# Turning attention scores onto their keys' partitions with a VectorE block transpose instead of TensorE transposes, with whole-chunk K buffers

## The chip, the cores and the metric

The kernel runs on one core of a Trainium2 chip. The metric is the time of one launch on the device, in microseconds (us). A core has five engines, which run side by side: TensorE (PE; its weight loads are listed apart as PEld), VectorE (DVE), ScalarE (ACT), GpSimd (POOL) and SyncE (SP, which here only issues DMA transfers). Sixteen DMA engines move data from memory (HBM) into SBUF. Matmul results land in PSUM.

## The reference, cut to what matters

One token is decoded: layer norm, attention over a cache of 65,536 keys with 32 query heads on 4 key/value heads, output projection, then layer norm and a gated feed-forward block.

```python
# x: 1x1x1024; k_cache, v_cache: 1x4x65536x128, bf16
q = x_normed @ wq                                    # 32 heads of 128
scores = einsum("bhqd,bhkd->bhqk", q, k) * 128**-0.5
p = softmax(scores)
o = einsum("bhqk,bhkd->bhqd", p, v)                  # then @ wo, + x
h2 = h + (gelu(hn @ w_gate) * (hn @ w_up)) @ w_down
```

K and V are 67 MB each, the weights about 39 MB. All of it must be read once: 173 MB.

## The kernel before: the parts that matter

All large loads share one pool of `NBUF = 5` buffers of 4 MB each. A load is issued when the buffer it reuses has been read for the last time.

```python
CW = 16384; NBUF = 5
chpool = ctx.enter_context(tc.tile_pool(name="chpool", bufs=NBUF))
def load(src, name):
    t = chpool.tile([P, CW], BF16, name=name, tag="ch")
    ...
    nc.sync.dma_start(out=tv, in_=src)
```

A K buffer is worked in four chunks of 32 keys per partition. Each chunk is transposed on TensorE (two neighbouring bf16 values of a key travel as one fp32 element), four blocks at a time into a PSUM bank, and copied out ("evicted") by ScalarE or VectorE. Then the query is multiplied with it. After two chunks the scores lie along the columns of a PSUM bank and have to be turned, so that each partition holds the scores of its own keys:

```python
for c in range(NBK):                                   # NBK = NB2 = 4
    kt_ps = ps_kt.tile([P, NB2, P], F32, ...)          # 3 PSUM banks
    for b in range(NB2):
        m0 = b * 8 + c * 2 + hf
        nc.tensor.transpose(out=kt_ps[:, b, :], in_=k32s[m0 // 16][:, m0 % 16, :], identity=ident_f[:])
    kt_sb = ktpool.tile([P, NB2, P], F32, ...)         # 6 buffers
    # evict kt_ps -> kt_sb on ACT or DVE
...
for par in range(2):
    for c in range(NBK):                               # column group c reads tile c
        nc.tensor.matmul(qk_ps[32*c:32*c+32, :], lhsT=qsel[:, g, par, hf, :], rhs=mv[:, :, :, par], ...)
...                                                    # after the second chunk of a pair:
nc.scalar.copy(out=qk_sb[:], in_=qk_ps[:])
for b in range(NB2):
    nc.tensor.transpose(out=sct_ps[:, b, :], in_=qk_sb[:, b*P:(b+1)*P], identity=ident_f[:])
nc.vector.tensor_copy(out=sl.rearrange("p h (m t) -> p m t h", t=2), in_=src_v)
nc.vector.tensor_reduce(out=st["mx"][:, :, pi], in_=sl, axis=AX.X, op=ALU.max)
```

When a head's K is done, the maximum is spread over the partitions and 16 exponentials on ScalarE make the probabilities. The V chunks of a head are interleaved with the K chunks of the next head.

## Time and profile before

| | before |
|---|---|
| time, median of the first 3 runs | 412.56 us (412.27 to 413.38) |
| span of the profiled run | 410.4 us |
| DMA bytes, mean rate | 173.43 MB, 423 GB/s |
| busy: PE, PEld, DVE, ACT | 296.6, 194.9, 168.2, 168.0 us |
| K load, issue to landing (median) | 27.3 us |

No engine's busy share says what bounds this kernel. The first thing to read is a table by stretch. The lines below, from the table of windows of the kernel before, give for each stretch (us from the start) its length, then the busy time of PE, PEld, DVE, ACT and POOL with instruction counts, then the granted TensorE clock (1.00 is full speed), the mean busy share of the 16 DMA engines, and what they moved in GB/s.

```profile
10.00:400.00 390.00, 290.19 (x2576) 189.71 (x2580) 165.87 (x283) 168.04 (x281) 3.57 (x7) 0.88 1.00 431
330.00:400.00 70.00, 38.63 (x353) 21.25 (x349) 7.11 (x29) 1.39 (x3) 2.17 (x4) 0.66 0.99 428
```

The DMA engines are busy throughout at 431 GB/s, and at nearly the same rate (428) from 330 to 400 us, where the other engines do little. So the rate does not come from what the engines do. (Single 10 us windows read up to 465 GB/s, with a DMA share of up to 1.08, so only long stretches are compared here.)

Whether the queue ever runs empty is the next question. These are the DMA issues of the page (size of one, median us from issue to landing).

```profile
k_sb<-in_A_k_cache_dram SPq DMA_DIRECT2D x16, 4096.0 KB, 27.3
v_sb<-in_A_v_cache_dram SPq DMA_DIRECT2D x16, 4096.0 KB, 21.7
```

A 4 MB load takes 4.19 MB / 431 GB/s = 9.7 us of the stream but 22 to 27 us from issue to landing, so it usually stands behind one or two others. How close it comes to running empty is read from the issues in order of time. This is the SP queue's timeline in head 0 (start, duration, transfer):

```profile
45.50 0.33 SPq L94 DMA_DIRECT2D v_sb<-in_A_v_cache_dram  x1
59.18 0.33 SPq L94 DMA_DIRECT2D k_sb<-in_A_k_cache_dram  x1
73.72 0.33 SPq L94 DMA_DIRECT2D v_sb<-in_A_v_cache_dram  x1
88.28 0.33 SPq L94 DMA_DIRECT2D k_sb<-in_A_k_cache_dram  x1
105.21 0.33 SPq L94 DMA_DIRECT2D v_sb<-in_A_v_cache_dram  x1
```

The stream needs a new load every 9.7 us. In head 0, where only K is worked, buffers come free every 13.7 to 14.6 us, and the fifth comes 17 us after the fourth: it waits for the first V matmuls, which wait for head 0's exponentials. The prefetched loads are the reserve that pays for this. I counted landings at 9.9 us per load from the start. By that count the load issued at 105.21 came about 6 us before the stream would have run dry.

Finally, the costliest groups (line, engine, operation, output<-inputs, shapes, count | busy us, mean ns | idle time before them and who ended it). Here and below, lines L223 to L321 are those of the kernel before.

```profile
L223 PE MATMUL kt_ps<-ident_f,k_sb 128*128 128x128 f32 x1024 | 148.2, 288 | 17.3 <-DVE kt_sb L230 12.9 <-DMA k_sb<-in_A_k_cache_dram 4.1 <-ACT kt_sb L228 0.2
...
L230 DVE COPY kt_sb<-kt_ps 128x1024 bf16<-128x1024 bf16 x140 | 94.7, 687 | 76.1 <-PE qk_ps L248 42.5 <-PE kt_ps L223 30.7
L248 PE MATMUL qk_ps<-kt_sb,qsel 128*32 128x512 bf16 x512 | 65.0, 395 | 7.7 <-DVE kt_sb L230 7.7
L259 DVE COPY sc_sb<-sct_ps 128x512 f32<-128x512 f32 x32 | 34.1, 1066 | 46.0 <-PE sct_ps L256 43.7 <-ACT kt_sb L228 2.3
...
L286 ACT ACTIVATE pT<-sc_sb,nbias 128x256 bf16<-128x256 f32 x64 | 31.5, 493 | 20.5 <-DVE nbias L278 20.5
L260 DVE TENSOR_REDUCE mx<-sc_sb 128x8 f32<-128x512 f32 x32 | 22.0, 687 | 1.0
L256 PE MATMUL sct_ps<-ident_f,qk_sb 128*128 128x128 f32 x128 | 19.9, 278 | 8.6 <-ACT qk_sb L253 8.6
L253 ACT COPY qk_sb<-qk_ps 128x512 f32<-128x512 f32 x32 | 18.8, 589 | 24.9 <-PE qk_ps L248 16.5 <-PE o_ps L319 8.3
```

L253, L256 and L259 are the three steps that turn the scores. L230 shows evictions that wait 42.5 us for QK matmuls: with six small buffers, the third and fourth eviction of a chunk need a buffer that the previous chunk's QK still reads.

The chain of waits (the work that ended last, followed back), by engine:

```profile
PE 52%; DMA 24%; DVE 14%; ACT 7%; issue 2%; SPq 0%; DVEq 0%; ACTq 0%
```

### The profile page before, as it was taken

The page shows a single profiled execution, that of the slowest core. Times are in us where ns is not written, and L with a number is a line of the kernel's source. Part 1 is how long each engine was busy: PE and PEld are TensorE (multiplying, and loading weights), DVE is VectorE, ACT ScalarE, POOL GpSimd, SP SyncE. Part 2 cuts the span into 40 slices and gives each one's busy share as a digit, 9 for nine tenths or more (in the row PEclk, how much of TensorE's full clock was granted, in tenths as well). Part 3 has the DMA queues.
Part 4 walks back from the last instruction along what each step waited for, and adds up shares of the span by engine and source line. Part 5 has one row for each costly group of instructions (what it writes and reads, how often), then busy time and mean ns, then how long its engine had stood idle before and what let it go on. Part 6 is the DMA issues. An engine that isn't in the chain of part 4 may idle for free.

```text
span 410.4 us, 6350 instructions
## 1 busy us (share of the span) xinstructions
PE 296.6 (72%) x2704; PEld 194.9 (47%) x2704; DVE 168.2 (41%) x296; ACT 168.0 (41%) x281; POOL 5.1 (1%) x16
## 2 busy tenths in 40 slices
PE   0438989889688987496988929888987466366366
PEld 0216656655366654464566617455654223163134
DVE  0213565557256545255556535456545101021011
ACT  0013766653855654733655634455744700000000
POOL 1100000000000000000000000000000001000000
PEclk9986999999999999599999966999999585668565
DMA  8999999999999999999999999999999999999994
GB/s 358 409 460 407 460 408 457 407 456 412 439 428 423 444 423 442 422 442 410 449 420 444 417 447 420 428 440 414 454 410 453 415 449 418 434 433 436 424 420 172
DMA packets 6684, 173.43 MB, mean 423 GB/s; under 512 B 896, under 2 KB 896, under 8 KB 1152
## 3 DMA queue, kind: packets, MB, share of 16 engines
q1 hardware_dynamic: 6496, 173.02, 98.1%
q8 instruction: 21, 0.34, 0.3%
q14 instruction: 7, 0.06, 0.0%
q10 hardware_dynamic: 160, 0.00, 0.0%
HBM read 173.02 MB, written 0.00 MB: 422 GB/s over the span
## 4 chain that ended last, share of the span: by engine, by line
PE 52%; DMA 24%; DVE 14%; ACT 7%; issue 2%; SPq 0%; DVEq 0%; ACTq 0%
PE kt_ps L223 27%; PE qk_ps L248 11%; DMA wd_sb<-in_B_w_down_dram 9%; DMA k_sb<-in_A_k_cache_dram 7%; DMA wo_sb<-in_A_wo_dram 7%; DVE sc_sb L259 6%; PE acc_ps L303 5%; ACT pT L286 5%; PE sct_ps L256 4%; DVE mx L260 4%; DVE kt_sb L230 3%; ACT qk_sb L253 2%; PE at_ps L361 1%; PE o_ps L319 1%; PE d_ps L361 1%
## 5 line engine op out<-in xcount | busy, mean ns | idle before, releaser
L223 PE MATMUL kt_ps<-ident_f,k_sb 128*128 128x128 f32 x1024 | 148.2, 288 | 17.3 <-DVE kt_sb L230 12.9
L228 ACT COPY kt_sb<-kt_ps 128x1024 bf16<-128x1024 bf16 x116 | 116.4, 1013 | 91.7 <-PE kt_ps L223 63.1
L223 PEld LDWEIGHTS kt_ps<-ident_f,k_sb 128*128 128x128 f32 x1024 | 117.6, 147 | 55.5 <-issue 21.3
L230 DVE COPY kt_sb<-kt_ps 128x1024 bf16<-128x1024 bf16 x140 | 94.7, 687 | 76.1 <-PE qk_ps L248 42.5
L248 PE MATMUL qk_ps<-kt_sb,qsel 128*32 128x512 bf16 x512 | 65.0, 395 | 7.7 <-DVE kt_sb L230 7.7
L259 DVE COPY sc_sb<-sct_ps 128x512 f32<-128x512 f32 x32 | 34.1, 1066 | 46.0 <-PE sct_ps L256 43.7
L286 ACT ACTIVATE pT<-sc_sb,nbias 128x256 bf16<-128x256 f32 x64 | 31.5, 493 | 20.5 <-DVE nbias L278 20.5
L303 PE MATMUL acc_ps<-v_sb,pT 128*32 128x512 bf16 x512 | 33.8, 408 | 3.8 <-DMA v_sb<-in_A_v_cache_dram 3.8
L253 ACT COPY qk_sb<-qk_ps 128x512 f32<-128x512 f32 x32 | 18.8, 589 | 24.9 <-PE qk_ps L248 16.5
L248 PEld LDWEIGHTS <-qsel 128*32 128x32 bf16 x512 | 15.1, 94 | 26.2 <-issue 23.9
L256 PE MATMUL sct_ps<-ident_f,qk_sb 128*128 128x128 f32 x128 | 19.9, 278 | 8.6 <-ACT qk_sb L253 8.6
L303 PEld LDWEIGHTS <-pT 128*32 128x32 bf16 x512 | 14.7, 102 | 18.7 <-issue 7.2
L260 DVE TENSOR_REDUCE mx<-sc_sb 128x8 f32<-128x512 f32 x32 | 22.0, 687 | 1.0
L256 PEld LDWEIGHTS sct_ps<-ident_f,qk_sb 128*128 128x128 f32 x128 | 14.3, 141 | 13.6 <-ACT qk_sb L253 13.6
L172 ACT COPY wg_ev<-wg_ps 96x512 f32<-96x512 f32 x1 | 0.6, 582 | 45.9 <-PE wg_ps L165 45.9
L312 PE MATMUL l_ps<-lpart,ones_f 128*128 128x8 f32 x16 | 3.7, 306 | 15.7 <-ACT pT L286 15.6
L165 PE MATMUL wu_ps<-wu_sb,hnz 128*32 128x512 bf16 x56 | 7.1, 620 | 9.7 <-DMA wu_sb<-in_B_w_up_dram 9.7
L165 PEld LDWEIGHTS <-hnz 128*32 128x32 bf16 x112 | 4.8, 123 | 17.8 <-issue 15.6
L361 PE MATMUL at_ps<-wo_sb,o2z 128*32 128x512 bf16 x64 | 6.6, 590 | 8.6 <-DMA wo_sb<-in_A_wo_dram 8.6
L286 ACT ACTIVATION_READ_ACCUMULATOR pT<-sc_sb,nbias 128x1 f32 x64 | 11.9, 187 | 0.0
L172 ACT ACT_TABLE_LOAD x1 | 1.3, 1283 | 25.0 <-DVE q_ev L170 25.0
L312 PEld LDWEIGHTS l_ps<-lpart,ones_f 128*128 128x128 f32 x16 | 3.0, 234 | 17.8 <-ACT pT L286 17.4
(125 smaller groups left out, 97.7 us busy)
## 6 DMA issues: line engine op xcount, KB each, us to landing
k_sb<-in_A_k_cache_dram SPq DMA_DIRECT2D x16, 4096.0 KB, 27.3
v_sb<-in_A_v_cache_dram SPq DMA_DIRECT2D x16, 4096.0 KB, 21.7
wq_sb<-in_A_wq_dram SPq DMA_DIRECT2D x2, 4096.0 KB, 16.7
wo_sb<-in_A_wo_dram SPq DMA_DIRECT2D x2, 4096.0 KB, 29.7
wg_sb<-in_B_w_gate_dram SPq DMA_DIRECT2D x2, 3584.0 KB, 33.1
wu_sb<-in_B_w_up_dram SPq DMA_DIRECT2D x2, 3584.0 KB, 40.6
wd_sb<-in_B_w_down_dram SPq DMA_DIRECT2D x1, 3584.0 KB
wd_sb<-in_B_w_down_dram SPq DMA_DIRECT2D x1, 1792.0 KB, 29.6
```

Source lines behind the costliest of these rows:

```text
L165: nc.tensor.matmul(banks[s // 4][32 * g:32 * g + 32, :], lhsT=stat, rhs=mov(s), start=first, stop=last, tile_position=(0, 32 * g))
L223: nc.tensor.transpose(out=kt_ps[:, b, :], in_=k32s[m0 // 16][:, m0 % 16, :], identity=ident_f[:])
L228: nc.scalar.copy(out=dst_bf, in_=src_bf)
L230: nc.vector.tensor_copy(out=dst_bf, in_=src_bf)
L248: nc.tensor.matmul(qk_ps[32 * c:32 * c + 32, :], lhsT=qsel[:, g, par, hf, :], rhs=mv[:, :, :, par], start=(hf == 0 and par == 0), stop=(hf ...
L253: nc.scalar.copy(out=qk_sb[:], in_=qk_ps[:])
L256: nc.tensor.transpose(out=sct_ps[:, b, :], in_=qk_sb[:, b * P:(b + 1) * P], identity=ident_f[:])
L259: nc.vector.tensor_copy(out=sl.rearrange("p h (m t) -> p m t h", t=2), in_=src_v)
L260: nc.vector.tensor_reduce(out=st["mx"][:, :, pi], in_=sl, axis=AX.X, op=ALU.max)
L286: nc.scalar.activation(out=pT[:, :, r, :], in_=sc_sb[:, r, hf * HG * TG:(hf + 1) * HG * TG].rearrange("p (a t) -> p a t", t=TG), func=ACT. ...
L303: nc.tensor.matmul(acc[32 * c:32 * c + rep * TG, :], lhsT=pTs[a // HG][:, a % HG, :, :].rearrange("p r t -> p (r t)"), rhs=v_sb[:, i * TG: ...
L361: nc.tensor.matmul(bank[32 * g:32 * g + 32, :], lhsT=stat, rhs=w2[:, s * 512:(s + 1) * 512], start=first, stop=last, tile_position=(0, 32 ...
```

## The change

The intent is to turn the scores with one VectorE 32x32 block transpose straight from PSUM. For that, column group c of the QK matmuls takes the keys of partitions 32c to 32c+31 of the whole chunk, so that the block transpose puts each score on its own partition. This drops a ScalarE copy, four TensorE transposes and the strided VectorE copy per pair of chunks, and frees a PSUM bank, which goes to the K transposes. Each chunk now has one large buffer, two in rotation. The scores lie key by key with the 8 heads side by side, so the maximum and the exponentials read at a step of 32 bytes. To make room in SBUF a small selector (`osel`) shares memory with the query tile and is built after attention.

```diff
-    ktpool = actx.enter_context(tc.tile_pool(name="ktpool", bufs=6))
+    ktpool = actx.enter_context(tc.tile_pool(name="ktpool", bufs=2))
-    ps_kt = actx.enter_context(tc.tile_pool(name="ps_kt", bufs=3, space=PSUM))
+    ps_kt = actx.enter_context(tc.tile_pool(name="ps_kt", bufs=4, space=PSUM))
-    ps_sct = actx.enter_context(tc.tile_pool(name="ps_sct", bufs=1, space=PSUM))
...                                        (osel moved; o_sb to another pool)
+        kt = ktpool.tile([P, NBK * NB2, P], F32, name="kt_sb", tag="kt")
-                m0 = b * 8 + c * 2 + hf
+                m0 = (c * NB2 + b) * 2 + hf
...
-            st["sc_sb"] = scpool.tile([P, rep, NT], F32, name="sc_sb", tag="sc")
+            st["sc_sb"] = scpool.tile([P, NT, rep], F32, name="sc_sb", tag="sc")
...
-                nc.tensor.matmul(qk_ps[32 * c:32 * c + 32, :], lhsT=qsel[:, g, par, hf, :], rhs=mv[:, :, :, par],
+                nc.tensor.matmul(qk_ps[32 * c:32 * c + 32, :], lhsT=qsel[:, g, par, hf, :],
+                                 rhs=mv[:, :, 32 * c:32 * c + 32, par],
...
-        nc.scalar.copy(out=qk_sb[:], in_=qk_ps[:])
-        for b in range(NB2):
-            nc.tensor.transpose(out=sct_ps[:, b, :], in_=qk_sb[:, b * P:(b + 1) * P], identity=ident_f[:])
-        nc.vector.tensor_copy(out=sl.rearrange("p h (m t) -> p m t h", t=2), in_=src_v)
-        nc.vector.tensor_reduce(out=st["mx"][:, :, pi], in_=sl, axis=AX.X, op=ALU.max)
+        sl = sc_sb[:, 2 * pi * CH:(2 * pi + 2) * CH, :]
+        nc.vector.transpose(out=sl.rearrange("p n h -> p (n h)"), in_=qk_ps[:])
+        nc.vector.tensor_reduce(out=st["mx"][:, :, pi], in_=sl.rearrange("p n h -> p h n"), axis=AX.X, op=ALU.max)
...
-                                     in_=sc_sb[:, r, hf * HG * TG:(hf + 1) * HG * TG].rearrange("p (a t) -> p a t", t=TG),
+                                     in_=sc_sb[:, hf * HG * TG:(hf + 1) * HG * TG, r].rearrange("p (a t) -> p a t", t=TG),
```

More of the change, by code (lines that the diff above doesn't have):

```diff
@@ L57 @@
     W2 = 2 * rep
-    assert NT % (DCH * CH) == 0 and CH % TG == 0 and CH == 32 and W2 == 16 and DCH % 2 == 0
+    assert NBK * NB2 * 32 == 512 and NT % (DCH * CH) == 0 and CH % TG == 0 and CH == 32 and W2 == 16 and DCH % 2 == 0
     lead = ctx.enter_context(tc.tile_pool(name="lead", bufs=1))
@@ L63 @@
     esel = lead.tile([P, 2, P], BF16, name="esel")
-    qsel = lead.tile([P, Hkv, 2, 2, 32], BF16, name="qsel")
+    qsel = lead.tile([P, Hkv, 2, 2, 32], BF16, name="qsel", tag="qo")
     hsel = lead.tile([P, 2], F32, name="hsel")
@@ L120 @@
             nc.vector.tensor_copy(out=esel[:, par, half * 64:(half + 1) * 64], in_=ident_bf[:, par::2])
-    OQ = P // Hq
-    osel = const.tile([Hq, OQ, P], BF16, name="osel")
-    nc.gpsimd.memset(osel[:], 0.0)
-    nc.gpsimd.affine_select(out=osel[:], in_=osel[:], compare_op=ALU.not_equal, fill=1.0, base=0,
-                            pattern=[[-1, OQ], [1, P]], channel_multiplier=-OQ)
     def layernorm_cols(src_col, dst_bf, tagp):
@@ L217, in k_chunk_T @@
         k32s = [k.rearrange("p n d -> p (n d)").bitcast(F32).rearrange("p (m e) -> p m e", e=Dh) for k in st["k_pair"]]
-        kts = []
+        kt = ktpool.tile([P, NBK * NB2, P], F32, name="kt_sb", tag="kt")
         for c in range(NBK):
@@ L221, in k_chunk_T @@
             for b in range(NB2):
-                m0 = b * 8 + c * 2 + hf
+                m0 = (c * NB2 + b) * 2 + hf
                 nc.tensor.transpose(out=kt_ps[:, b, :], in_=k32s[m0 // 16][:, m0 % 16, :], identity=ident_f[:])
-            kt_sb = ktpool.tile([P, NB2, P], F32, name="kt_sb", tag="kt")
             src_bf = kt_ps[:].rearrange("p b k -> p (b k)").bitcast(BF16)
-            dst_bf = kt_sb[:].rearrange("p b k -> p (b k)").bitcast(BF16)
+            dst_bf = kt[:, c * NB2:(c + 1) * NB2, :].rearrange("p b k -> p (b k)").bitcast(BF16)
             if act_for(g, ci, c):
@@ L230, in k_chunk_T @@
                 nc.vector.tensor_copy(out=dst_bf, in_=src_bf)
-            kts.append(kt_sb)
-        st[("kt", ci)] = kts
+        st[("kt", ci)] = kt
     def k_chunk_QK(g, ci):
@@ L236, in k_chunk_QK @@
         pi, hf = divmod(ci, 2)
-        kts = st.pop(("kt", ci))
+        kt = st.pop(("kt", ci))
         if ci == 0:
-            st["sc_sb"] = scpool.tile([P, rep, NT], F32, name="sc_sb", tag="sc")
+            st["sc_sb"] = scpool.tile([P, NT, rep], F32, name="sc_sb", tag="sc")
             st["mx"] = small.tile([P, rep, NCH // 2], F32, name="mx", tag="mx")
@@ L244, in k_chunk_QK @@
         qk_ps = st["qk_ps"]
+        mv = kt[:].rearrange("p b k -> p (b k)").bitcast(BF16).rearrange("p (b k t) -> p b k t", b=NBK * NB2, t=2)
         for par in range(2):
-            for c in range(NBK):
-                mv = kts[c][:].rearrange("p b k -> p (b k)").bitcast(BF16).rearrange("p (b k t) -> p b k t", b=NB2, t=2)
-                nc.tensor.matmul(qk_ps[32 * c:32 * c + 32, :], lhsT=qsel[:, g, par, hf, :], rhs=mv[:, :, :, par],
+            for c in range(4):
+                nc.tensor.matmul(qk_ps[32 * c:32 * c + 32, :], lhsT=qsel[:, g, par, hf, :],
+                                 rhs=mv[:, :, 32 * c:32 * c + 32, par],
                                  start=(hf == 0 and par == 0), stop=(hf == 1 and par == 1), tile_position=(0, 32 * c))
@@ L251, in k_chunk_QK @@
             return
-        qk_sb = qkpool.tile([P, NB2 * P], F32, name="qk_sb", tag="qk")
-        nc.scalar.copy(out=qk_sb[:], in_=qk_ps[:])
-        sct_ps = ps_sct.tile([P, NB2, P], F32, name="sct_ps", tag="sctps")
-        for b in range(NB2):
-            nc.tensor.transpose(out=sct_ps[:, b, :], in_=qk_sb[:, b * P:(b + 1) * P], identity=ident_f[:])
-        src_v = sct_ps[:].rearrange("p b x -> p (b x)").rearrange("p (m t h) -> p m t h", t=2, h=rep)
-        sl = sc_sb[:, :, 2 * pi * CH:(2 * pi + 2) * CH]
-        nc.vector.tensor_copy(out=sl.rearrange("p h (m t) -> p m t h", t=2), in_=src_v)
-        nc.vector.tensor_reduce(out=st["mx"][:, :, pi], in_=sl, axis=AX.X, op=ALU.max)
+        sl = sc_sb[:, 2 * pi * CH:(2 * pi + 2) * CH, :]
+        nc.vector.transpose(out=sl.rearrange("p n h -> p (n h)"), in_=qk_ps[:])
+        nc.vector.tensor_reduce(out=st["mx"][:, :, pi], in_=sl.rearrange("p n h -> p h n"), axis=AX.X, op=ALU.max)
         if ci == NCH - 1:
@@ L337 @@
         v_chunk(Hkv - 1, ci)
+    OQ = P // Hq
     assert Hq * OQ == P and Dh == OQ * Hq
+    osel = lead.tile([Hq, OQ, P], BF16, name="osel", tag="qo")
+    nc.gpsimd.memset(osel[:], 0.0)
+    nc.gpsimd.affine_select(out=osel[:], in_=osel[:], compare_op=ALU.not_equal, fill=1.0, base=0,
+                            pattern=[[-1, OQ], [1, P]], channel_multiplier=-OQ)
     o_ps = ps_m.tile([Hq, Dh], BF16, name="oh_ps", tag="misc")
     nc.tensor.transpose(out=o_ps[:], in_=oT_all[:], identity=ident_bf[:])
-    o_sb = small.tile([Hq, Dh], BF16, name="o_sb", tag="o_sb")
+    o_sb = const.tile([Hq, Dh], BF16, name="o_sb")
     nc.vector.tensor_copy(out=o_sb[:], in_=o_ps[:])
```

## The prediction

> **What bounds the kernel now.** The DMA stream. The page's DMA row shows a busy share of 0.9 or more in 38 of 40 slices and 173.43 MB over a 410.4 us span. In the table of 10 us windows the DMA share is 0.97 to 1.08 and the rate 419 to 465 GB/s in every window from 10 to 400 us, equally where the compute engines are half idle (330 to 400 us: 423 to 435 GB/s). The Trainium skill, "DMA: Bandwidth & Descriptors", section "Where 436 GB/s comes from", puts the fabric ceiling at 435 GB/s; the trace agrees: 173.4 MB up to about 402 us is 431 GB/s. And transfers are always queued: the SP queue's waits show K and V loads waiting for buffers (242.7 us on QK, 55.3 us on the V matmuls), but a 4 MB load takes about 9.9 us at that rate, while the median from issue to landing is 27.3 us for K and 21.7 us for V. Counting 9.9 us per load, the tightest issues (105, 184.5 and 262 us, after each head's softmax) still come about 6 to 8 us before the stream would run dry.
>
> The chain of waits names PE for 52% and DMA for 24%; I take that as hand-offs paced by the stream, not as the bound.
>
> **What the change does** (32 chunk pairs):
> - ACT loses the score copies: 32 x 0.589 = 18.8 us.
> - PE loses 128 score transposes: 19.9 us matmul busy, 14.3 us weight loads.
> - DVE: the 1.066 us copy becomes a 32x32 block transpose of 128x512 fp32 from PSUM. A plain copy of that shape from PSUM takes 0.692 us here (acc_sb); I expect 0.6 to 0.8 us, so DVE loses 9 to 15 us.
> - The maximum and the exponentials now read scores at a 32-byte step. Today they take 687 and 493 ns. The Trainium skill, "SBUF — State Buffer" (16-byte cachelines), says that such a step pays a penalty; no reading in this trace shows how much. I expect 0 to 40%.
> - Two whole-chunk buffers replace six quarter-chunk ones, so evictions need not wait for the QK matmuls before them (42.5 us of DVE and 28.7 us of ACT idling in the waits view).
>
> In head 0, where only K is used, a 4 MB buffer is released every 14.5 us. I expect 12 to 13.5 us after.
>
> **How much is on the critical path.** Nearly none. Faster release moves buffer-free times earlier, so loads wait longer in the DMA queue; the stream stays at 420 to 460 GB/s. The first load, the start, and the tail after the last w_down piece (about 404 to 410 us) are untouched. The selector moved to the end of attention runs near 325 us, before wo lands (about 355 us).
>
> **Prediction: 412.2 us, range 410.5 to 414.2. Chances: faster 0.03, same 0.94, slower 0.03.**
>
> **What the profile would show.** DMA share still 0.97 or more in every window from 10 to 400 us; K issue to landing longer than 27.3 us; ACT busy about 149 us and DVE about 156 us if the strided reads cost nothing; PE matmul busy down by about 20 us or more; the head-0 release interval shorter; end of the last w_down matmuls within 2 us of 407.
>
> **What would make it wrong.** Exponentials at twice their time or more, or a block transpose over 1.5 us: a head's end would lengthen by more than the 6 us reserve and the stream would run dry there (slower). Or the stream is not at its ceiling: then the earlier issues would lift GB/s (faster).

## The result, and the profile after

| | before | after |
|---|---|---|
| time, median of 4 runs | 412.50 us | 412.47 us (412.21 to 412.63) |
| ratio after / before | | 0.9995 (95%: 0.9977 to 1.0012): same |
| span of the profiled run | 410.4 us | 410.6 us |
| busy: PE, DVE, ACT | 296.6, 168.2, 168.0 us | 272.3, 169.5, 163.0 us |
| mean granted TensorE clock | 0.875 | 0.803 |

Ratios here and below are the mean time of one kernel's fast runs over that of the other's in the same rounds, so not quite the ratio of the medians.

The windows of the changed kernel (columns as above) show less PE time and the same stream:

```profile
10.00:400.00 390.00, 265.90 (x2448) 188.67 (x2452) 167.11 (x283) 163.01 (x249) 4.04 (x8) 0.81 1.00 431
330.00:400.00 70.00, 37.88 (x301) 20.86 (x304) 7.08 (x28) 1.39 (x3) 0.56 (x1) 0.57 1.00 430
```

The DMA issues of the changed kernel: a load now stands in the queue for 38 to 40 us instead of 22 to 27.

```profile
k_sb<-in_A_k_cache_dram SPq DMA_DIRECT2D x16, 4096.0 KB, 40.0
v_sb<-in_A_v_cache_dram SPq DMA_DIRECT2D x16, 4096.0 KB, 37.6
```

And its SP queue in head 0, as above. Buffers come free every 11.2 us instead of about 14.5, and the first load after head 0's end is issued at 95.74 instead of 105.21 us:

```profile
43.38 0.33 SPq L93 DMA_DIRECT2D v_sb<-in_A_v_cache_dram  x1
54.59 0.33 SPq L93 DMA_DIRECT2D k_sb<-in_A_k_cache_dram  x1
65.79 0.33 SPq L93 DMA_DIRECT2D v_sb<-in_A_v_cache_dram  x1
77.00 0.33 SPq L93 DMA_DIRECT2D k_sb<-in_A_k_cache_dram  x1
95.74 0.33 SPq L93 DMA_DIRECT2D v_sb<-in_A_v_cache_dram  x1
```

So the compute part did become faster. It also now waits for data, as the costliest groups show (lines L216 to L289 are those of the changed kernel; L216 is the K transpose, L222 the VectorE eviction, L272 the exponential, L246 the maximum, L245 the block transpose):

```profile
L216 PE MATMUL kt_ps<-ident_f,k_sb 128*128 128x128 f32 x1024 | 144.7, 304 | 37.2 <-DMA k_sb<-in_A_k_cache_dram 34.2 <-DVE kt_sb L222 3.0
...
L222 DVE COPY kt_sb<-kt_ps 128x1024 bf16<-128x1024 bf16 x140 | 95.3, 688 | 92.8 <-PE kt_ps L216 89.8
L272 ACT ACTIVATE pT<-sc_sb,nbias 128x256 bf16<-128x256 f32 x64 | 47.6, 745 | 23.7 <-DVE nbias L264 23.7
L239 PE MATMUL qk_ps<-kt_sb,qsel 128*32 128x512 bf16 x512 | 39.7, 384 | 9.9 <-ACT kt_sb L220 9.2 <-DVE kt_sb L222 0.7
...
L246 DVE TENSOR_REDUCE mx<-sc_sb 128x8 f32<-128x512 f32 x32 | 35.2, 1099 | 0.5
L245 DVE STREAM_TRANSPOSE sc_sb<-qk_ps 128x512 f32<-128x512 f32 x32 | 23.0, 717 | 19.1 <-PE qk_ps L239 18.8 <-ACT pT L272 0.3
```

PE idled 34.2 us before K transposes for K to land; in the kernel before that was 4.1 us. The VectorE evictions no longer wait for QK. The strided reads have a price: the maximum went from 687 to 1099 ns, the exponential from 493 to 745 ns.

The chain of waits of the changed kernel has moved from PE to DMA:

```profile
DMA 51%; PE 21%; ACT 5%; DVE 4%; issue 1%; DVEq 0%
```

In both kernels attention ends with V matmuls that wait for the last V load, within 0.2 us of each other. The lines are from the two timelines, before first:

```profile
336.64 3.61 PE L303 MATMUL acc_ps<-v_sb,pT 128*32 128x512 bf16 x32 [3.84 <-DMA v_sb<-in_A_v_cache_dram]
```

```profile
336.45 3.60 PE L289 MATMUL acc_ps<-v_sb,pT 128*32 128x512 bf16 x32 [7.17 <-DMA v_sb<-in_A_v_cache_dram]
```

The rest of both runs is the weights other than `wq`, less what is already prefetched, at the same rate.

### The profile page after: what moved, and what is told of

It reads as the page before. It is cut to its first block, busy times and chain, and to the rows that moved or that the text cites. A ratio compares the mean times of both kernels' runs of the same rounds, so it can differ in the third digit from the quotient of the medians.

```text
span 410.6 us, 6002 instructions
## 1 busy us (share of the span) xinstructions
PE 272.3 (66%) x2576; PEld 193.8 (47%) x2576; DVE 169.5 (41%) x296; ACT 163.0 (40%) x249; POOL 5.1 (1%) x16
## 4 chain that ended last, share of the span: by engine, by line
DMA 51%; PE 21%; ACT 5%; DVE 4%; issue 1%; DVEq 0%
DMA k_sb<-in_A_k_cache_dram 27%; PE kt_ps L216 13%; DMA wu_sb<-in_B_w_up_dram 10%; DMA v_sb<-in_A_v_cache_dram 10%; DMA wd_sb<-in_B_w_down_dram 5%; ACT pT L272 4%; PE qk_ps L239 3%; PE acc_ps L289 2%; ACT kt_sb L220 2%; DVE mx L246 1%; PE wu_ps L158 1%; DVE kt_sb L222 1%; DVE sc_sb L245 1%; PE o_ps L305 1%; PE bc_ps L262 0%
## 5 line engine op out<-in xcount | busy, mean ns | idle before, releaser
L216 PE MATMUL kt_ps<-ident_f,k_sb 128*128 128x128 f32 x1024 | 144.7, 304 | 37.2 <-DMA k_sb<-in_A_k_cache_dram 34.2
L216 PEld LDWEIGHTS kt_ps<-ident_f,k_sb 128*128 128x128 f32 x1024 | 131.7, 159 | 57.8 <-issue 36.5
L220 ACT COPY kt_sb<-kt_ps 128x1024 bf16<-128x1024 bf16 x116 | 111.9, 1015 | 105.4 <-issue 74.7
L222 DVE COPY kt_sb<-kt_ps 128x1024 bf16<-128x1024 bf16 x140 | 95.3, 688 | 92.8 <-PE kt_ps L216 89.8
L272 ACT ACTIVATE pT<-sc_sb,nbias 128x256 bf16<-128x256 f32 x64 | 47.6, 745 | 23.7 <-DVE nbias L264 23.7
L239 PE MATMUL qk_ps<-kt_sb,qsel 128*32 128x512 bf16 x512 | 39.7, 384 | 9.9 <-ACT kt_sb L220 9.2
L289 PE MATMUL acc_ps<-v_sb,pT 128*32 128x512 bf16 x512 | 37.4, 441 | 12.1 <-DMA v_sb<-in_A_v_cache_dram 12.1
L246 DVE TENSOR_REDUCE mx<-sc_sb 128x8 f32<-128x512 f32 x32 | 35.2, 1099 | 0.5
L245 DVE STREAM_TRANSPOSE sc_sb<-qk_ps 128x512 f32<-128x512 f32 x32 | 23.0, 717 | 19.1 <-PE qk_ps L239 18.8
L289 PEld LDWEIGHTS <-pT 128*32 128x32 bf16 x512 | 17.2, 107 | 28.4 <-issue 19.7
L239 PEld LDWEIGHTS <-qsel 128*32 128x32 bf16 x512 | 8.4, 94 | 24.4 <-DVE kt_sb L222 15.2
L298 PEld LDWEIGHTS l_ps<-lpart,ones_f 128*128 128x128 f32 x16 | 3.2, 250 | 24.0 <-ACT pT L272 23.1
L302 DVE COPY acc_sb<-acc_ps 128x512 f32<-128x512 f32 x4 | 2.7, 684 | 22.6 <-PE acc_ps L289 22.6
L272 ACT ACTIVATION_READ_ACCUMULATOR pT<-sc_sb,nbias 128x1 f32 x64 | 12.0, 187 | 0.0
```

What stands on the lines that cost most here:

```text
L220: nc.scalar.copy(out=dst_bf, in_=src_bf)
L222: nc.vector.tensor_copy(out=dst_bf, in_=src_bf)
L239: nc.tensor.matmul(qk_ps[32 * c:32 * c + 32, :], lhsT=qsel[:, g, par, hf, :], rhs=mv[:, :, 32 * c:32 * c + 32, par], start=(hf == 0 and pa ...
L245: nc.vector.transpose(out=sl.rearrange("p n h -> p (n h)"), in_=qk_ps[:])
L246: nc.vector.tensor_reduce(out=st["mx"][:, :, pi], in_=sl.rearrange("p n h -> p h n"), axis=AX.X, op=ALU.max)
L272: nc.scalar.activation(out=pT[:, :, r, :], in_=sc_sb[:, hf * HG * TG:(hf + 1) * HG * TG, r].rearrange("p (a t) -> p a t", t=TG), func=ACT. ...
```

## The experiments

Theory: the stream of 173 MB binds; the change shortens the compute part by tens of us, all of which goes into longer queues. Rival A: the change's gain was real and on the path, and the strided reads gave it back. Rival B: compute paces the stream, so that less compute would let it run faster. A further question is what the freed compute time is good for.

A warning on correctness: with these inputs attention's part in the output is too small for the comparison to see. So that comparison does not vouch for the changed score layout; for that I rely on following the indices through the code (column 32b + 16·hf + 8·t + h of the bank becomes key 4b + 2·hf + t, head h).

### 1. The stream alone

```diff
-    for g in range(Hkv):  ...  k_chunk_T / k_chunk_QK / v_chunk
+    nc.vector.memset(oT_all[:], 0.0)
+    for g in range(Hkv):
+        for ci in range(NCH):
+            kv_dma(k_v[g], ci, "k_sb")
+            if g >= 1:
+                kv_dma(v_v[g - 1], ci, "v_sb")
+    for ci in range(NCH):
+        kv_dma(v_v[Hkv - 1], ci, "v_sb")
```

> The changed kernel with every K and V load kept and all attention arithmetic on them taken out (the result is wrong on purpose). Theory 'the stream is the bound': no attention work at all changes nothing, 411 to 413 us, DMA share 0.97 or more until about 400 us. Rival 'compute paces the stream, and the change's gain was given back by the strided reads': the time falls well below 405 us.

Measured: 409.6 us (409.51 to 409.87), ratio to before 0.9927 (0.9911 to 0.9944). The windows line:

```profile
10.00:400.00 390.00, 43.64 (x349) 22.62 (x349) 10.27 (x47) 3.26 (x5) 4.07 (x8) 0.54 1.00 432
```

With all attention arithmetic gone, PE busy falls from 290 us in the kernel before (266 in the changed kernel, on which this run is built) to 44 us in this stretch, the DMA share stays at 1.00, the rate goes from 431 to 432 GB/s, and the launch is 2.9 us shorter. That is 1.4 us below the range I had written. All attention arithmetic therefore costs about 0.7% of the time, and rival B falls. The gain comes before the last weights land: the first matmuls on `w_down` start at 395.52 us instead of 398.29. Part of it may be instruction fetch, which the profile pages count on the same 16 DMA engines. These are the instruction queues of the pages, before and then stream alone (packets, MB, share of 16 engines):

```profile
q8 instruction: 21, 0.34, 0.3%
q14 instruction: 7, 0.06, 0.0%
```

```profile
q8 instruction: 3, 0.05, 0.0%
...
q14 instruction: 1, 0.01, 0.0%
```

0.3% of 410 us is 1.2 us, as an estimate; no run changed the fetch alone. The other 1.7 us stay open.

### 2. The compute part alone, before and after

Each head loads its first K and V buffer only and uses it four times, so 24 of 32 loads (101 MB) are gone and the arithmetic is unchanged. The order of TensorE's instructions shifts somewhat, because the scheduler sees fewer loads, so these times compare variants and are not exact parts of the full kernel's time.

```diff
-        key = (name, id(src_v), bi)
-        if si == 0:
-            kv_big[key] = load(src_v[:, bi * DCH * CH:(bi + 1) * DCH * CH, :], name)
-        tv = kv_big[key] if si < DCH - 1 else kv_big.pop(key)
+        key = (name, id(src_v))
+        if ci == 0:
+            kv_big[key] = load(src_v[:, 0:DCH * CH, :], name)
+        tv = kv_big[key] if ci < NCH - 1 else kv_big.pop(key)
```

> The kernel before, but each head loads only its first K and its first V buffer and uses it four times (wrong on purpose): 24 of 32 loads, 101 MB, are gone, the arithmetic is the same. Now compute should bind. From the trace of before: 105 us to the first V release, then 3 heads of about 75 us, then a tail of about 40 us: 355 to 375 us. Rival 'before has much hidden slack': below 340 us.

> The same cut of loads in the changed kernel. Theory 'the change did shorten compute, but off the critical path': 315 to 340 us, that is 30 to 50 us under cut_before. Rival 'strided reads gave the gain back': within 5 us of cut_before.

Measured: cut_before 346.35 us (345.1 to 346.6), cut_after 301.21 us (299.86 to 302.88). Both are lower than I had expected; the difference, 45.1 us, is in the range. The change takes 13% off the time when compute binds. Rival A, in the form that the strided reads gave the gain back, falls. The kernel before was not far from being bound by compute: 346 us against 410 for the stream. These times include a tail in which the weights stream again, about 42 us after the last V matmuls in both; the gain lies before it, where those matmuls end at 302.9 and 258.0 us. With all loads they end at 340 us in both kernels.

### 3. Which part of the change makes compute faster

cut_before_kt8 gives the kernel before eight quarter-chunk buffers instead of six (with the selector moved, to make room) and keeps the TensorE turn of the scores:

```diff
-    ktpool = actx.enter_context(tc.tile_pool(name="ktpool", bufs=6))
+    ktpool = actx.enter_context(tc.tile_pool(name="ktpool", bufs=8))
```

> cut_before (loads cut to 8, wrong on purpose) with eight quarter-chunk buffers in place of six, the selector moved to make room as in the changed kernel, and everything else as before: the change's buffering without its block transpose. In cut_before DVE idled 36.8 us and ACT 27.3 us in evictions that waited for QK. If the buffering is the main part of the 45 us between cut_before and cut_after: 305 to 325 us. If the removed transposes and copies are: 330 to 344 us. I lean to 325 to 338, a share for each.

Measured: 324.29 us (323.02 to 325.29). This is just under the range that I leaned to, and just inside the first one; the split is about half and half. The buffering alone is worth 22.1 us of the 45.1; the block transpose, the new QK mapping and the fourth PSUM bank together give the other 23.1, after paying for the strided reads. No run separates these three, or makes them without the buffering. The waits view of the cut kernel before, and then with eight buffers (who waited for whom: us, times, longest), shows the mechanism (L225, L223 and L218 are L230, L228 and L223 in the numbering of that kernel):

```profile
DVE kt_sb L230 <- PE qk_ps L248: 36.8, 29, 1.5
...
ACT kt_sb L228 <- PE qk_ps L248: 27.3, 53, 1.0
```

```profile
DVE kt_sb L225 <- PE kt_ps L218: 76.3, 63, 6.4
ACT kt_sb L223 <- PE kt_ps L218: 52.5, 75, 7.3
```

With eight buffers the evictions wait for the transposes that feed them and no longer for QK.

### 4. The price of the strided reads

perm_after and cut_perm_after let the block transpose write with a step instead, so that each head's scores lie together as before:

```diff
-            st["sc_sb"] = scpool.tile([P, NT, rep], F32, name="sc_sb", tag="sc")
+            st["sc_sb"] = scpool.tile([P, rep, NT], F32, name="sc_sb", tag="sc")
-        nc.vector.transpose(out=sl.rearrange("p n h -> p (n h)"), in_=qk_ps[:])
+        nc.vector.transpose(out=sl.rearrange("p h n -> p n h"), in_=qk_ps[:].rearrange("p (n h) -> p n h", h=rep))
...                                        (maximum and exponentials read without a step)
```

> cut_after, but the block transpose writes its scores at a stride so that each head's scores lie next to each other, as in the kernel before; the maximum and the exponentials then read without a step. Expected: exponentials back from 745 to about 493 ns, maximum from 1099 to about 687 ns, the transpose up from 717 to about 1070 ns (as the strided copy of before had it); 64 exponentials at 0.25 us less, 16 us in all, stand in a row at each head's end, so 8 to 16 us under cut_after. If strided reads cost nothing on the compute path: the same as cut_after.

> The changed kernel with all loads and five buffers, its scores written at a stride so that they are read without one; in the cut pair this took 16 us off. Theory 'the stream binds': 412 to 412.8 us, same as the kernel before. Rival 'the strided reads gave back a gain': below 404 us.

Measured: cut_perm_after 284.98 us (284.11 to 285.39), 16.2 us under cut_after; perm_after 412.53 us, ratio to before 1.0001 (0.9985 to 1.0017). The groups of cut_perm_after:

```profile
L245 DVE STREAM_TRANSPOSE sc_sb<-qk_ps 128x512 f32<-128x512 f32 x32 | 34.7, 1083 | 11.3 <-PE qk_ps L239 8.7 <-ACT pT L272 2.5
L272 ACT ACTIVATE pT<-sc_sb,nbias 128x256 bf16<-128x256 f32 x64 | 31.5, 494 | 23.4 <-DVE nbias L264 23.4
L246 DVE TENSOR_REDUCE mx<-sc_sb 128x8 f32<-128x512 f32 x32 | 21.6, 674 | 0.5
```

On VectorE the step only changes hands: the transpose goes from 717 to 1083 ns, the maximum from 1098 to 674 ns. On ScalarE 64 exponentials save 254 ns each, 16.3 us in all, about the 16.2 us of the whole. Where the stream binds, this further gain is also worth nothing, and rival A falls a second time: with the penalty on the exponentials taken away, the full kernel still takes 412.5 us.

### 5. Fewer load buffers: spending the reserve

If the freed time sits in the queue as reserve, then taking 4 MB buffers away must hurt the kernel before first. The edit is one number; the TensorE instruction order stays the same as with five buffers (the traces list the same 2704 matmuls, 2576 in the changed kernel, in the same order with five, four and three).

```diff
-    NBUF = 5
+    NBUF = 4
```

> The kernel before with four 4 MB buffers in place of five (result right). Its tightest loads were issued 6 to 8 us before the stream would run dry; one buffer less takes about 9.9 us of that. Theory 'the reserve is what the change buys': the stream runs dry a few us at each head's end, 417 to 430 us. Rival 'the reserve plays no part': 412 to 413 us.

> The changed kernel with four buffers (result right). Its tightest K or V load was issued about 16 us ahead of the stream, so one buffer less still leaves about 6 us: theory 411 to 414 us, and faster than nbuf4_before. Rival: same as nbuf4_before.

> The kernel before with three buffers: the reserve falls to about -14 us at each of four head ends: 445 to 480 us.

> The changed kernel with three buffers: reserve about -4 us at each head's end: 420 to 440 us, at least 15 us under nbuf3_before.

| load buffers | kernel before | changed kernel |
|---|---|---|
| 5 | 412.50 us | 412.47 us |
| 4 | 422.09 us, ratio 1.0235 (1.022 to 1.025) | 412.38 us, ratio 1.0000 (0.9985 to 1.0015) |
| 3 | 442.30 us, ratio 1.0712 (1.069 to 1.0735) | 421.11 us, ratio 1.0218 (1.0184 to 1.0252) |

The ratios are to the kernel before with five buffers. With four buffers the two kernels differ by 2.3%; with five they are the same. The dry spell is visible in the windows at the end of head 0, first in the kernel before with four buffers, then in the changed one:

```profile
90.00:100.00 10.00, 9.60 (x69) 5.99 (x67) 7.56 (x15) 2.54 (x9) 0.00 (x0) 1.00 0.96 408
100.00:110.00 10.00, 7.40 (x67) 4.82 (x67) 1.59 (x3) 9.21 (x30) 0.00 (x0) 0.89 0.56 215
```

```profile
90.00:100.00 10.00, 6.79 (x67) 3.97 (x68) 3.22 (x6) 8.07 (x17) 0.00 (x0) 0.83 0.99 429
100.00:110.00 10.00, 9.24 (x88) 7.15 (x88) 8.27 (x12) 7.23 (x8) 0.00 (x0) 1.00 0.97 418
```

In the kernel before with four buffers the DMA share falls to 0.56 from 100 to 110 us. I had expected a dry spell at each head's end. There are two, and neither is at a later head's end: one at head 0's end (10 GB/s from 100 to 105 us) and a shorter one after it (213 GB/s from 125 to 130 us). This fits the later head ends: they hardly moved (first issue at 185.52 us against 184.51 with five buffers), while the stream was by then about 9 us behind, which is worth about the missing buffer. From 100 to 150 us the mean rate was 367 GB/s against 430 with five buffers, which is 50 x (1 - 367/430) = 7.3 us of the 9.4 us by which the span grew. With three buffers the kernel before lost less than I had expected, 30 us rather than 33 to 68.

> The same eight quarter-chunk buffers in the full kernel before, with four 4 MB buffers (result right). nbuf4_before took 422.1 us, about 10 us of it from one dry spell at the end of head 0. If the buffering alone shortens a head by a few us, part of it comes back: 414 to 420 us; if it alone suffices, 412.5 us.

Measured: 421.15 us (420.32 to 421.95), outside the range: almost nothing came back, although the same buffering was worth 22 us in the cut pair. The timelines of the SP queue show why, first nbuf4_before and then nbuf4_before_kt8:

```profile
87.48 0.33 SPq L94 DMA_DIRECT2D v_sb<-in_A_v_cache_dram  x1
104.42 0.33 SPq L94 DMA_DIRECT2D k_sb<-in_A_k_cache_dram  x1
110.80 0.33 SPq L94 DMA_DIRECT2D v_sb<-in_A_v_cache_dram  x1
```

```profile
84.32 0.33 SPq L94 DMA_DIRECT2D v_sb<-in_A_v_cache_dram  x1
108.34 0.33 SPq L94 DMA_DIRECT2D k_sb<-in_A_k_cache_dram  x1
109.12 0.33 SPq L94 DMA_DIRECT2D v_sb<-in_A_v_cache_dram  x1
```

Head 0 finishes its K 3 us earlier, but the next load is issued 4 us later. After head 0 two buffers are due, head 1's first K buffer and head 0's first V buffer. In nbuf4_before the V matmuls stand in a row and free theirs at 104.4 us, before the K buffer (110.8). In nbuf4_before_kt8 they come after the second half of the exponentials and are spread between K transposes, QK matmuls and score transposes in TensorE's fixed order, so that the K buffer is free at 108.3 and the V buffer at 109.1 us. A faster average pace did not help, since the one release that mattered came no earlier. The windows agree: the second dry spell is gone (416 GB/s from 125 to 130 us), but the first is longer (3 GB/s from 100 to 105 us and 105 from 105 to 110, where nbuf4_before is back at 419). I read this from the timelines and the SP queue's waits; no run changed that order alone.

> nbuf3_after (421.1 us) with the strided writes in place of strided reads (result right). The 16 exponentials at each head's end take 4 us less, the dry spell at the end of head 0 shrinks by about that: 414 to 418 us. If head ends were not what drains the reserve: 421 us.

Measured: 417.5 us (416.67 to 418.26), against 421.1 us with strided reads: 3.6 us, about the 16 x 0.25 = 4.0 us by which the exponentials at one head's end become shorter. This agrees with the dry spell at the end of head 0 as what sets the loss: from 90 to 100 us the stream moved 121 GB/s with strided reads and 218 without, which at 430 GB/s is about 2.3 us of it (an estimate).

No version beats both kernels. The stream-alone run says how little could be had: with these loads issued in this way, taking out all of the attention arithmetic gives 409.6 us.

## Why the prediction was right

- **The time.** Predicted 412.2 us (410.5 to 414.2), measured 412.47, and "same" at 0.94 came true. This time could not test the compute terms below: perm_after, with 16 us less compute by the cut pair, takes the same 412.5 us.
- **The stream as the bound.** Right. Experiment 1 shows it directly: no attention arithmetic, 0.7% less time. The Trainium skill, "DMA: Bandwidth & Descriptors", section "Where 436 GB/s comes from", gives 435 GB/s as the fabric ceiling; 431 to 432 GB/s from 10 to 400 us agrees with it. Which part of the path from memory sets this rate, no run here shows.
- **Nearly none on the critical path; loads wait longer in the queue.** Right: K issue to landing went from 27.3 to 40.0 us.
- **The chain of waits.** I read its "PE 52%" as hand-offs paced by the stream. That was too quick. Experiment 2 put the kernel before at 346 us with most loads gone, and experiment 5 shows that one buffer less exposes its compute. It sat close to both bounds, and the chain was right to pass through compute for long stretches. After the change the chain is 51% DMA and 21% PE, with the time unchanged: the chain names a path that ended last, not how much is gained by shortening it.
- **The block transpose.** Predicted 0.6 to 0.8 us, measured 0.717. Right. PE matmul busy fell by 24.3 us, predicted 20 or more.
- **The strided reads.** Predicted 0 to 40% slower; measured 1099/687 = 1.60 and 745/493 = 1.51. The term was mis-sized. The Trainium skill, "SBUF — State Buffer", section "Specifications (TRN2)", says that each crossing to a new 16-byte line pays a penalty but not how much; these runs agree that there is one at a 32-byte step. So DVE busy rose by 1.3 us and ACT fell by 5.0 us; the falls to about 156 and 149 us had been forecast for strided reads that cost nothing.
- **The release interval in head 0.** Predicted 12 to 13.5 us, measured 11.2; the direction was right and the size too small.
- **The reserve.** Predicted about 6 to 8 us at the head ends; the packet records give 5.2, 3.6 and 4.1 us, so the estimate was somewhat high. As it implies, taking away one buffer, worth about 10 us, made the stream dry at head 0's end. My later expectation that it would also run dry at the other heads' ends was wrong.

## What to carry to other kernels

Before making compute cheaper, ask how long a load stands in the queue and how full the stream is: here 173 MB at 431 GB/s left 0.7% for everything in attention. A change off the critical path still buys reserve, and the reserve can be spent: after this change the kernel holds its time with four load buffers instead of five, which frees 32 KB per partition (16,384 bf16 elements). To value such a change, take away the bound (fewer loads) or the reserve (fewer buffers) in both kernels, and compare there.

## What the Trainium skill lacked or had wrong

- "DMA: Bandwidth & Descriptors", section "Where 436 GB/s comes from": it says that the HBM side (about 358 GB/s) binds HBM-to-SBUF transfers, without saying there for how many cores. With this kernel on one core, 432 GB/s was held from 10 to 400 us. "Perfetto Trace Analysis", section "Roofline", has it right for one active core (about 435 GB/s).
- "SBUF — State Buffer": no size for the 16-byte-line penalty on VectorE or ScalarE. Measured for fp32 at a 32-byte step: VectorE maximum over 128x512, 687 to 1099 ns; ScalarE exponential over 128x256, 493 to 745 ns. Writing at a step of 2 KB (512 fp32) took the VectorE block transpose from 717 to 1083 ns.
- "VectorE: DVE Perf Modes", section "The three transpose paths": one VectorE figure, for 128x128 bf16. Measured for 128x512 fp32 from PSUM to SBUF: 717 ns, against 684 to 692 ns for a plain copy of that shape.
- "TensorE: Matmul & The Clock Gate", section "Part 1: The HAM clock gate (the "warmup" mystery)", says that the clock falls to half after idle time. This is not wrong, and the runs agree: the granted clock was 0.54 from 10 to 400 us with the stream alone, where PE was busy for 44 of 390 us. What can be added is how it reads. In the changed kernel, which waits more for data, the mean granted clock fell from 0.875 to 0.803 and the same K transposes show a mean of 304 instead of 288 ns, at an unchanged total time. So a mean matmul duration that grows is not by itself a sign of a worse kernel.
